# One core, attention into routed experts: a new table of priorities, group scores in one order of the array, value products by 64 columns, and small copies for two engines

## The chip, the core and the metric

One core of a Trainium2 chip runs the whole kernel. TensorE (PE in the rows, PEld for its loads of the stationary operand), VectorE (DVE), ScalarE (ACT) and GpSimd (POOL) each work through a list of instructions of their own, in a fixed order, and wait for each other by semaphores; SyncE (SP) issues most DMAs. The metric is the device time in microseconds from start to end of one execution.

## The reference, cut to what matters

The first half is attention over 8 batches of 8 heads, with 512 local and 32 global positions of 64 numbers each. Local rows see a band of 32 to either side and the global keys; global rows see all. The second half sends the result, as 544 rows of 512 numbers per batch, through four experts with causal attention, of which each row keeps two.

```python
s_g = scale * np.matmul(q_g, k_all.transpose(0, 1, 3, 2))
out_g = np.matmul(sm(s_g), v_all)
mask = np.abs(pos[:, None] - pos[None, :]) <= window          # window = 32
a_l = sm(np.concatenate([s_lg, np.where(mask, s_ll, -1e9)], axis=-1))
out_l = np.matmul(a_l, np.concatenate([v_g, v_l], axis=2))
...
for e in range(E):                                            # 4 experts, 2 of them kept per row
    q, k, v = x @ wq[e], x @ wk[e], x @ wv[e]
    ye = softmax(causal(scale * q @ k.transpose(0, 2, 1))) @ v @ wo[e]
    out += gate[e] * ye
```

All is float32. A float32 product stands in the rows of the trace as two instructions of TensorE, so a matmul of the program counts twice there; the projections split their operands into a high and a low part of a shorter type (`xh`, `xl`) and count once for each product of parts.

## The kernel before, in words

The 32 pairs of heads (8 batches of 4 pairs) go through the first half one after the other, in steps; the experts' work of a batch is laid between the pairs of later ones, and `step` writes down, for each step, what belongs to it. For pair k: `p1_load` and `p1_load_values` fetch it, `p1_trans` makes the transposed keys `kd` and queries `qp`, `p1_scores` (32 matmuls on tiles of 64 rows by 32 columns of the array) and `p1_softmax` make the banded weights, `p1_ptrans` turns them on TensorE, `p1_av` multiplies with the values `v` (tiles of 128 rows by 32 columns), `p1_turn` turns the result into `xh` and `xl`.

Around the values much is copied: `p1_load_values` builds overlapping windows of `v` from one loaded copy by six moves between partitions (`move`; one of them, of the last window alone, is small: 32x128) and three copies of the global values (`vg`). Before, all nine run on GpSimd, as do the copy of the global keys into `kd` in `p1_trans` and four copies `xt<-xh`, `xt<-xl` per batch in `m_v`. In a row of the trace they all bear the line of the helper `copy` (L417) or their own (L668, L1020).

Two pairs make a group, whose 128 global queries against 544 keys need a softmax of their own. In steps 1 and 3, and where the experts' tail rows of an older batch have scores in the same step, `long_scores` does it: 12 matmuls, four tiles of the array at a time. In the eight other groups `split_scores` (L838) cuts the keys into parts of 320 and 224 and lays them on all eight tiles at once; its softmax then has to swap minima and sums between the halves of the partitions (`swap`, L850) with small VectorE instructions, and has two exponentials on ScalarE (L860) for one (L934).

The experts of a batch: `m_v`, `m_qk` project (128x128 tiles), `m_gates` picks two of four, `m_scores`, `m_softmax`, `m_ptrans` as above, `m_av` (L1237) multiplies with the values in 32 columns of the array at a time, four tiles side by side, `m_out` and `m_out_tail` project and write 128x512 tiles; the last tile is written in two halves.

The order on each engine is no loop's: `Plan.op` writes down every operation with a duration that the author gives it and a priority (the step times 100, plus a shift from the table `SHIFT`), and `Plan.place` then plays the whole kernel through and fixes on every engine the order in which operations could start. An operation with two engines (`"ACT|DVE"`) gets the one that is free first. `SHIFT` is looked up by the function that an operation belongs to, its duration and its step.

Of the kernel before, what the change touches and what calls it, by code (L numbers as in the profile page):

```python
# [49 lines left out]
class Op:  # L50
    def __init__(self, k, engs, ns, fn, prio, packets, shape, slow, code, flow):
# [13 lines left out]
LAND = 650.0  # L65
# [10 lines left out]
SHARE = 800.0  # L76

SWITCH = {"scores": 198.0, "av": 114.0, "turn": 143.0}
# [10 lines left out]
    "clear_banks": {(3500, 100): -200},  # L89
    "evac": {(180, 100): -250, (180, 103): -50, (266, 110): 130, (266, 118): 120, (276, 116): 20,  # L90
        (316, 102): -110, (316, 108): 220, (369, 114): -120, (448, 103): 110, (475, 100): -240, (475, 102): -100,
        (475, 105): -90, (475, 106): -110, (475, 108): -140, (475, 112): -80, (475, 113): -70, (475, 135): 80},
    "high_low": {(264, 133): -100, (332, 104): -250, (332, 107): 140, (332, 111): 50, (332, 124): 160,
        (332, 130): -90, (332, 133): -70, (598, 113): 140, (598, 139): 250},
    "load": {(550, 100): -250, (550, 101): -250, (550, 102): -250, (550, 106): -220, (550, 108): -70,
        (550, 109): -70, (550, 123): -50, (550, 124): -140},
    "long_scores": {(60, 101): -240, (60, 103): -130, (60, 135): -200, (80, 111): -180, (80, 119): -50,
        (80, 127): -70, (80, 131): -90, (880, 101): -220, (880, 103): -170, (880, 111): -180, (880, 119): -50,
        (880, 123): -40, (880, 127): -20, (880, 131): -60, (880, 135): -250},
    "m_av": {(680, 141): -160, (1560, 141): -250, (2220, 113): -70, (2220, 115): -40, (2220, 117): -50,  # L100
        (2220, 121): -190, (2220, 123): -100, (2220, 125): -150, (2220, 127): 70, (2220, 129): -110,
        (2220, 133): -140, (2220, 135): -220},
    "m_gates": {(440, 115): -130, (440, 131): 180, (630, 115): 160, (1300, 111): 60},
    "m_qk": {(1504, 107): 80, (1504, 112): -60, (1504, 116): -10, (1504, 119): 10, (1504, 120): -70,
        (1504, 123): -50, (1504, 124): -30, (1504, 127): -120, (1504, 128): -20, (1504, 136): 250},
    "m_scores": {(431, 108): -100, (431, 110): 80, (431, 114): 30, (431, 116): 70, (431, 118): 50,
# [5 lines left out]
    "m_softmax": {(80, 120): -80, (80, 124): 80, (211, 111): -90, (211, 115): 140, (211, 133): -130,  # L112
# [4 lines left out]
    "m_tail_av": {(583, 113): 110, (583, 117): -50, (583, 121): 90, (583, 129): -10, (583, 133): -70,  # L117
        (583, 137): 190, (583, 141): -180},
    "m_tail_softmax": {(100, 131): 80, (110, 111): 150, (110, 119): 120, (610, 115): -90, (610, 119): -80,
        (610, 127): -30, (610, 139): -110, (745, 115): -110},  # L120
    "m_v": {(1440, 105): 50, (1440, 110): -150, (1440, 114): 60, (1440, 118): -50, (1440, 126): -90,
        (1440, 130): -40, (1440, 134): 250},
    "m_v_tails": {(330, 111): -60, (330, 119): 110, (1062, 111): -250},
    "out_tile": {(1400, 113): 60, (1400, 117): -80, (1400, 121): 150, (1400, 125): -110, (1400, 129): -100,
# [45 lines left out]
class Plan:  # L170
# [5 lines left out]
    def __init__(self):  # L176
        self.ops = []
        self.writers = {}
        self.prio = 0
# [183 lines left out]
def fused_kernel(ctx: ExitStack, tc: tile.TileContext, q_l, k_l, v_l, q_g, k_g, v_g,  # L363
# [1022 lines left out]
    def step(s):  # L1386
# [9 lines left out]
        def local():  # L1396
# [4 lines left out]
            elif group or tail is not None:  # L1401
                long_scores(group, tail)
# [120 lines left out]
```

## Time and profile before

| | |
|---|---|
| time, median of 3 runs | 463.72 us (463.31 to 464.33) |
| the profiled execution | 464.11 us, of which its span 462.3 us |
| busy: TensorE, VectorE, ScalarE, GpSimd | 443.6, 384.2, 329.4, 291.7 us |
| TensorE's granted clock | 1.0 of full speed throughout |

The profiled execution is 0.4 us above the median; 1.8 us of it lie around the span. TensorE is busy for 96% of the span, but "busy" holds pipelined instructions whose ends are modelled, so a stretch with full busy time can still hold gaps. How long a piece of TensorE's work takes is better read from the starts: from the first instruction of one piece to the first of the next.

### The profile page before, as it was taken

Reading aid. Unit: us, or ns where it says so; the run is one execution under the profiler, and the core shown is the slowest. Engines: PE = TensorE matmul, PEld = TensorE weight load, DVE = VectorE, ACT = ScalarE, POOL = GpSimd, SP = SyncE. Lnnn points to the kernel's source line nnn. Section 1 sums busy time; section 2 is a strip of 40 time slices with the busy share of each in tenths; the row PEclk is TensorE's granted clock in tenths of the full one; section 3 lists DMA queues with packets and bytes.
Section 4 is the critical chain, followed back from the end, with each engine's and each line's share of the span. In section 5 each row is a group of like instructions: output and inputs, shape, how many; then the busy total and the mean of one; then the engine's idle time right before and its main releaser. Section 6 shows DMA issues by size and latency. Waiting matters only on the chain.

```text
span 462.3 us, 25861 instructions
## 1 busy us (share of the span) xinstructions
PE 443.6 (96%) x10572; PEld 385.6 (83%) x10572; DVE 384.2 (83%) x1714; ACT 329.4 (71%) x1198; POOL 291.7 (63%) x563
## 2 busy tenths in 40 slices
PE   7877899999999999999999999999999999999996
PEld 5666789898879988789888898899978998798875
DVE  6997989999996997798988899598997986476681
ACT  4977759676886777786877688579678794563582
POOL 8899887998687559658409696744854931340420
PEclk9999999999999999999999999999999999999999
DMA  8786665865346345553135733653305000300023
GB/s 179 171 188 117 124 119 103 157 107 109 55 105 143 66 77 107 129 89 63 20 57 106 171 64 59 160 101 70 60 3 148 5 4 3 94 3 1 26 72 115
DMA packets 182535, 41.01 MB, mean 89 GB/s; under 512 B 177680, under 2 KB 177936, under 8 KB 182416
## 3 DMA queue, kind: packets, MB, share of 16 engines
q1 hardware_dynamic: 181840, 38.57, 40.6%
q8 instruction: 83, 1.36, 1.3%
q10 hardware_dynamic: 576, 0.79, 0.6%
q14 instruction: 36, 0.29, 0.2%
HBM read 30.42 MB, written 8.91 MB: 85 GB/s over the span
## 4 chain that ended last, share of the span: by engine, by line
PE 82%; DVE 6%; POOL 5%; issue 2%; SPq 2%; ACT 1%; DMA 1%; DVEq 0%; POOLq 0%; ACTq 0%
PE bank L998 20%; PE bank L739 11%; PE bank L1310 10%; PE bank L1029 9%; PE bank L1237 7%; PE bank L1151 6%; PE bank L769 6%; PE bank L706 5%; POOL v L417 5%; PE bank L968 2%; SPq L432 2%; PE bank L909 1%; PE bank L1291 1%; PE bank L838 1%; PE bank L800 1%
## 5 line engine op out<-in xcount | busy, mean ns | idle before, releaser
L417 POOL COPY v<-v 32x512 f32<-32x512 f32 (+3 forms) x192 | 114.3, 595 | 21.2 <-DMA v<-in_v_l_dram 11.7
L1186 POOL TENSOR_SCALAR pm<-pm,msm,gate 128x256 f32<-128x256 f32 (+3 forms) x124 | 74.7, 616 | 72.5 <-DVE msm L1175 24.9
L721 ACT ACTIVATE st<-st,sm 128x128 f32<-128x128 f32 x256 | 99.6, 392 | 16.4 <-DVE sm L718 16.3
L1170 ACT ACTIVATE pm<-pm,msm 128x128 f32<-128x128 f32 (+3 forms) x128 | 70.9, 557 | 26.0 <-DVE msm L1166 25.6
L417 POOL COPY v<-vg 32x640 f32<-32x640 f32 (+1 forms) x96 | 68.5, 714 | 11.7 <-issue 3.6
L718 DVE CUSTOM_DVE_ANT_0 st<-bank,band 128x128 f32<-128x128 f32 x256 | 58.0, 284 | 2.2 <-PE bank L706 1.8
L721 ACT ACTIVATION_READ_ACCUMULATOR st<-st,sm 128x1 f32 x256 | 48.6, 190 | 0.0
L706 PE MATMUL bank<-kd,qp 64*32 64x128 f32 x2048 | 39.4, 272 | 2.5 <-issue 1.4
L1166 DVE CUSTOM_DVE_ANT_0 pm<-bank,cmask 128x512 f32<-128x512 f32 (+1 forms) x64 | 38.0, 612 | 3.1 <-PE bank L1151 2.9
L1151 PE MATMUL bank<-kt,qt 64*32 64x480 f32 (+15 forms) x1024 | 38.7, 394 | 0.5 <-issue 0.5
L998 PE MATMUL bank<-xh,wk_hi 128*128 128x272 f32 x128 | 38.6, 302 | 0.0
L769 PE MATMUL bank<-v,ptw 128*32 128x64 f32 x2048 | 35.6, 220 | 3.0 <-POOL v L417 2.0
L706 PEld LDWEIGHTS bank<-kd,qp 64*32 64x32 f32 x2048 | 33.0, 105 | 6.3 <-issue 3.6
L1029 PE MATMUL bank<-wv_hi,xh 128*128 128x260 f32 x128 | 37.2, 291 | 0.0
L998 PE MATMUL bank<-xl,wk_hi 128*128 128x272 f32 x128 | 37.0, 289 | 0.0
L998 PE MATMUL bank<-xh,wq_hi 128*128 128x272 f32 x128 | 37.0, 289 | 0.0
L998 PE MATMUL bank<-xh,wq_lo 128*128 128x272 f32 x128 | 36.9, 289 | 0.0
L998 PE MATMUL bank<-xh,wk_lo 128*128 128x272 f32 x128 | 36.8, 288 | 0.0
L998 PE MATMUL bank<-xl,wq_hi 128*128 128x272 f32 x128 | 36.8, 287 | 0.0
L769 PEld LDWEIGHTS bank<-v,ptw 128*32 128x32 f32 x2048 | 31.4, 110 | 6.2 <-POOL v L417 2.6
L1029 PE MATMUL bank<-wv_lo,xh 128*128 128x260 f32 x128 | 36.3, 283 | 0.0
L1029 PE MATMUL bank<-wv_hi,xl 128*128 128x260 f32 x128 | 36.1, 282 | 0.1
(194 smaller groups left out, 1300.5 us busy)
## 6 DMA issues: line engine op xcount, KB each, us to landing
v<-in_v_l_dram SPq DMA_DIRECT2D x64, 120.0 KB, 3.0
kn<-in_k_l_dram SPq DMA_DIRECT2D x104, 64.0 KB, 2.5
qn<-in_q_l_dram SPq DMA_DIRECT2D x104, 64.0 KB, 2.5
out_dram<-ot SPq DMA_DIRECT2D x66, 64.0 KB, 1.7
out_dram<-ot SPq DMA_DIRECT2D x14, 256.0 KB, 2.4
v<-in_v_l_dram SPq DMA_DIRECT2D x32, 64.0 KB, 2.7
kn<-in_k_l_dram SPq DMA_DIRECT2D x12, 128.0 KB, 3.2
qn<-in_q_l_dram SPq DMA_DIRECT2D x12, 128.0 KB, 3.3
```

What stands on the lines that cost most here:

```text
L417: ENG[e].tensor_copy(out, in_)
L706: nc.tensor.matmul(sp[h].t[32 * g:32 * g + 32, 128 * t:128 * t + 128], qp.t[rows, 32 * u:32 * u + 32], kd.t[rows, c:c + 128], start=True, ...
L718: op("DVE", 211, lambda e, h=h, t=t, i=i: nc.vector.tensor_tensor_reduce(out=st.t[:, h, t], in0=sp[h].t[:, 128 * t:128 * t + 128], in1=ban ...
L721: op("ACT", 385, lambda e, h=h, t=t, i=i: nc.scalar.activation(st.t[:, h, t], st.t[:, h, t], AF.Exp, bias=sm.t[:, 0, i:i + 1], scale=-1.0, ...
L739: nc.tensor.transpose(two[y].t[:, k, :], block()[rows], ident[rows, rows])
L769: nc.tensor.matmul(xq.t[32 * g:32 * g + 32, t, h, :], pt.t[:, h, 32 * u:32 * u + 32], v.t[:, h, window(u), :], start=True, stop=True)
L998: nc.tensor.matmul(pp.t, w[:, ch, cols], x(part, ch)[:, n], start=(ch == 0 and w is hi and part == 0), stop=(ch == NCH - 1 and part == 1))
L1029: nc.tensor.matmul(pv.t, x(part, ch)[:, 128 * i:128 * i + 128], w[:, ch, :], start=(ch == 0 and part == 0 and w is hi), stop=(ch == NCH - ...
L1151: nc.tensor.matmul(sp[x].t[32 * g:32 * g + 32, at:at + n], qt.t[rows, q0:q0 + 32], kt.t[rows, :n], start=True, stop=True)
L1170: op("ACT", 280 + 0.83 * n, lambda e, x=x, at=at, n=n, s=s: nc.scalar.activation(pm.t[:, x, at:at + n], pm.t[:, x, at:at + n], AF.Exp, bia ...
L1186: lambda e, x=x, at=at, n=n, row=row, s=s: ENG[e].tensor_scalar(pm.t[:, x, at:at + n], pm.t[:, x, at:at + n], sm.t[:, 3, s:s + 1], gate.t[ ...
L1310: nc.tensor.matmul(po.t, lhs(part, c), w[:, c, :], start=(c == 0 and part == 0 and w is hi), stop=(c == 1 and part == 1))
```

## The change

It has five parts.

1. `SHIFT` is a new table. Its keys name an operation more closely: helpers (`evac`, `load`, `turn_halves`, ...) by the function that they serve (`owner`), and on TensorE and SyncE also by how many of the same kind came before in the step (`#0`, `#1`). The table's numbers are new, and so are many of the durations and constants by which `Plan.place` plays the kernel through.
2. `split_scores` is gone; all groups go through `long_scores` and `p1_global_softmax`.
3. `m_av` takes 64 columns of the array at a time: half as many matmuls, two tiles side by side.
4. The small window move, the copy into `kd` and the four `xt` copies may go to GpSimd or VectorE.
5. The multiply of the experts' weights keeps its engines, but has other durations in the plan.

```diff
 SHIFT = {
-    "clear_banks": {(3500, 100): -200},
+    "clear_banks#0": {(3500, 100): -160},
+    "evac into long_turn": {(316, 120): -70, (316, 126): -110},
...
-        kind = fn.__code__.co_qualname.split(".<locals>.")[1]
+        kind = owner(fn)
         step = int(self.prio // 100)
+        key = kind, round(ns[0]), step
+        if engs[0] in ("PE", "SP"):
+            self.seen[key] = self.seen.get(key, -1) + 1
+            kind += f"#{self.seen[key]}"
...
-            op(*spread(252 + 0.79 * 128 * cols, 2 * D * cols), f, r=[(v, key)], w=[(v, ("m", to, slots.start, frm))], late=120)
+            engs, ns = spread(252 + 0.79 * 128 * cols, 2 * D * cols) if cols > 1 else ("POOL|DVE", (655, 200))
+            op(engs, ns, f, r=[(v, key)], w=[(v, ("m", to, slots.start, frm))], late=120)
...
-        op("POOL", 380, lambda e: nc.gpsimd.tensor_copy(
-            groups(kd.t)[:, :, 96:], kq.t[:, p:p + 1, :SG].to_broadcast([128, n3, SG])), r=[kq], w=[(kd, "g")])
+        op("POOL|DVE", (640, 240), lambda e: copy(
+            e, groups(kd.t)[:, :, 96:], kq.t[:, p:p + 1, :SG].to_broadcast([128, n3, SG])), r=[kq], w=[(kd, "g")])
...
-    def split_scores(b, g):
...
-        op("PE", 580, f, r=[kq, *kdl], w=sps, shape="scores", code=64, flow=0.8)
...
-                    op("POOL", 300, lambda e, g=g, k=k, part=part: nc.gpsimd.tensor_copy(
-                        xt.t[:, 2 * g:2 * g + 2, b % 2, k, :], X[b, g, part].t[:, :, SL:]), r=[X[b, g, part]],
+                    op("POOL|DVE", (540, 150), lambda e, g=g, k=k, part=part: copy(
+                        e, xt.t[:, 2 * g:2 * g + 2, b % 2, k, :], X[b, g, part].t[:, :, SL:]), r=[X[b, g, part]],
...
-                            for d in range(0, D, 32):
-                                nc.tensor.matmul(yp.t[64 * x + d:64 * x + d + 32, at:at + width],
-                                                 vt.t[:, j, 64 * (2 * c + x) + d:64 * (2 * c + x) + d + 32],
-                                                 pt.t[:, x, 2 * j:2 * j + width // 128, :].rearrange("p s q -> p (s q)"),
-                                                 start=(j == 0), stop=(j == big))
+                            nc.tensor.matmul(yp.t[64 * x:64 * x + 64, at:at + width],
+                                             vt.t[:, j, 64 * (2 * c + x):64 * (2 * c + x) + 64],
+                                             pt.t[:, x, 2 * j:2 * j + width // 128, :].rearrange("p s q -> p (s q)"),
+                                             start=(j == 0), stop=(j == big))
...
-            if group and tail is None and s >= 5:
-                split_scores(*group)
-            elif group or tail is not None:
+            if group or tail is not None:
                 long_scores(group, tail)
```

Over the whole program VectorE gets 21 of the 32 small moves, 12 of the 32 copies into `kd` and 15 of the 32 `xt` copies; with `split_scores` 40 small VectorE instructions go (64 of its own against 24 of the one softmax, the two evacuations left out on both sides). TensorE's tile shape changes 173 times instead of 166; away from the 64x32 shape of the scores it changes 36 times instead of 39.

Here is GpSimd, early in the program, at the values of the fourth pair, the last of the first batch; `kd_77` is the key tile of a later pair, `cmask` a mask of the experts, `xt` a copy that waits for the first group's result. Before:

```order
L417 COPY v<-vg 32x10x64 x2
L417 COPY v<-vg 32x2x4x64
L417 COPY v<-v 32x10x64 x2
L417 COPY v<-v 32x2x4x64
L417 COPY v<-v 32x2x64
L417 COPY v<-v 32x2x4x64
L417 COPY v<-v 64x2x4x64
L668 COPY kd_77<-kq 128x5x32
```

And after, up to the same last move of that pair:

```order
L478 COPY v<-vg 32x10x64 x2
L478 COPY kd_77<-kq 128x5x32
L567 MEMSET cmask 128x512
L568 AFFINE_SELECT cmask<-cmask 128x128
L478 COPY xt<-xh 128x2x32
L478 COPY xt<-xl 128x2x32
L478 COPY v<-v 32x10x64 x2
L478 COPY v<-v 32x2x4x64 x2
L478 COPY v<-v 64x2x4x64
```

The small move (32x2x64) has left the row, as in the three pairs ahead; the mask, which before stood in front of all values, and two `xt` copies have come in front of the last moves.

TensorE at the third group, before (`kd_78` and `kd_79` are its two pairs' keys; the rows go on in this manner to 16):

```order
L838 MATMUL bank_68<-kd_78,kq 32x192
L838 MATMUL bank_70<-kd_78,kq 32x32
L838 MATMUL bank_68<-kd_79,kq 32x192
L838 MATMUL bank_70<-kd_79,kq 32x32
L838 MATMUL bank_68<-kd_78,kq 32x192
L838 MATMUL bank_70<-kd_78,kq 32x32
```

After, where the same group's keys are `kd_78` and `kd_77`, and the score tile of a pair follows at once:

```order
L903 MATMUL bank_66<-kd_78,kq 32x128 x2
L903 MATMUL bank_66<-kd_77,kq 32x128 x2
L903 MATMUL bank_66<-kd_78,kq 32x384 x2
L903 MATMUL bank_66<-kd_77,kq 32x384 x2
L768 MATMUL bank_68<-kd_77,qp 32x128
```

The wide half of the group stands alone in four matmuls of 128 and four of 384 columns; its last four, of 32 columns, stand elsewhere in the row.

ScalarE at the very end, before:

```order
L415 COPY ot<-bank_69 128x512
L1324 DMA out_dram<-ot 128x512
L1324 DMA out_dram<-ot 32x512 x2
L415 COPY ot<-bank_64 128x256
L1319 DMA out_dram<-ot 128x256
```

After:

```order
L476 COPY ot<-bank_71 128x512
L1324 DMA out_dram<-ot 32x512 x4
L476 COPY ot<-bank_70 128x256
L1319 DMA out_dram<-ot 128x256
L1324 DMA out_dram<-ot 128x512
```

The tile that is written in halves is no longer the last: a whole tile, evacuated by VectorE in one piece, is issued behind it.

## Rows read from the trace of the kernel before

**Rows 1.** Busy time by stretch: us, PE, PEld, DVE, ACT, POOL, clock, DMA.

```profile
0.00:42.00 42.00, 32.84 (x983) 24.90 (x983) 34.66 (x158) 30.48 (x115) 37.50 (x82) 1.00 0.78 169
42.00:140.00 98.00, 94.41 (x2352) 84.03 (x2356) 92.62 (x423) 73.21 (x281) 82.69 (x152) 1.00 0.59 110
140.00:380.00 240.00, 238.51 (x5940) 211.86 (x5939) 208.10 (x950) 182.97 (x677) 152.19 (x293) 1.00 0.40 81
```

**Rows 2.** TensorE in order of time: start, us, what, [idle before <- releaser]; early.

```profile
9.96 1.13 PE L901 MATMUL bank<-kd,kq 64*32 64x32 f32 x24
11.02 0.66 PE L676 MATMUL bank<-ident,kn 128*128 128x128 f32 x4
12.05 1.16 PE L706 MATMUL bank<-kd,qp 64*32 64x128 f32 x64
13.13 0.71 PE L739 MATMUL bank<-ident,st 64*128 64x64 f32 x16
...
37.25 1.03 PE L769 MATMUL bank<-v,ptw 128*32 128x64 f32 x57 [1.38 <-POOL v L417]
...
41.60 0.38 PE L706 MATMUL bank<-kd,qp 64*32 64x128 f32 x2 [0.38 <-issue]
```

**Rows 3.** GpSimd in order of time, the first 40 us.

```profile
6.26 0.52 POOL L506 MEMSET cmask<- 128x512 f32 x1
...
9.20 1.91 POOL L417 COPY v<-vg 32x512 f32<-32x512 f32 x3 [0.17 <-DMA vg<-in_v_g_dram]
11.17 0.32 POOL L668 COPY kd<-kq 128x160 f32<-128x160 f32 x1
...
12.96 7.63 POOL L417 COPY v<-v 32x640 f32<-32x640 f32 x12 [0.70 <-DMA v<-in_v_l_dram]
...
29.14 4.21 POOL L417 COPY v<-vg 32x640 f32<-32x640 f32 x3
...
37.52 0.23 POOL L1020 CAST xt<-xh 128x64 fp32r<-128x64 f32 x1
```

**Rows 4.** TensorE in order of time, from 60 us.

```profile
62.52 1.16 PE L706 MATMUL bank<-kd,qp 64*32 64x128 f32 x64
63.42 0.83 PE L838 MATMUL bank<-kd,kq 64*32 64x192 f32 x32
63.96 1.42 PE L1151 MATMUL bank<-kt,qt 64*32 64x416 f32 x32
...
78.97 0.66 PE L739 MATMUL bank<-ident,st 64*128 64x64 f32 x16
79.46 0.88 PE L739 MATMUL bank<-ident,pm 64*128 64x64 f32 x16
...
84.12 0.40 PE L706 MATMUL bank<-kd,qp 64*32 64x128 f32 x2 [1.05 <-issue]
```

**Rows 5.** Waits of TensorE: who for whom, us in total, times, longest.

```profile
PEld bank L1237 <- issue: 1.8, 5, 0.8
...
PE bank L739 <- ACT long L860: 1.2, 1, 1.2
```

**Rows 6.** The chain that ended last: start, us, what.

```profile
105.20 2.16 PE bank L1237 x48
```

**Rows 7.** VectorE and GpSimd at 67.4 us, in order of time.

```profile
67.39 0.72 POOL L417 COPY v<-vg 32x640 f32<-32x640 f32 x1
...
67.41 0.73 DVE L724 TENSOR_SCALAR sm<-sm 128x8 f32<-128x8 f32 x1
```

**Rows 8.** Groups by shape: count, busy us, mean ns of one, idle before.

```profile
L724 DVE TENSOR_SCALAR sm<-sm 128x8 f32<-128x8 f32 x32 | 9.7, 302 | 3.3 <-ACT st L721 3.3
...
L417 POOL COPY v<-v 32x128 f32<-32x128 f32 x32 | 9.3, 292 | 1.8
```

**Rows 9.** DMA issues: count, KB each, us from issue to landing.

```profile
out_dram<-ot ACTq DMA_DIRECT2D x1, 256.0 KB, 2.1
...
out_dram<-ot ACTq DMA_DIRECT2D x1, 128.0 KB, 1.8
```

More of the change, by code (lines that the diff above doesn't have):

```diff
@@ L64 @@
 START = 500.0
-LAND = 650.0
+LAND = 700.0
 AGAIN = 700.0
@@ L75 @@
 HELD = 150.0, 400.0
-SHARE = 800.0
-SWITCH = {"scores": 198.0, "av": 114.0, "turn": 143.0}
+SHARE = 500.0
+SWITCH = {"scores": 225.0, "av": 114.0, "turn": 143.0}
 ENTER = 105.0
@@ L95 @@
[L95 to L102, printed above, removed]
@@ new lines @@
+    "evac into long_turn": {(316, 120): -70, (316, 126): -110},
+    "evac into p1_ptrans": {(475, 102): -210},
+    "evac m_ptrans": {(369, 112): -150, (369, 140): -250},
+    "evac out_tile": {(475, 129): 80},
+    "evac p1_batch_turn": {(262, 110): -40, (262, 126): -90},
+    "evac p1_trans": {(180, 101): -140, (448, 100): 60, (448, 101): -190, (448, 102): -160, (448, 103): 30,
+        (475, 102): -250, (475, 103): -190},
+    "high_low m_av": {(477, 137): -30, (598, 133): -250},
[24 rows of a table added]
+    "m_gates": {(450, 119): 250, (630, 131): 250, (700, 119): 110},
[13 rows of a table added]
@@ new lines, with owner @@
+    "m_softmax": {(211, 111): 40, (211, 123): 70, (211, 139): 30, (344, 128): 140, (386, 125): 140,
[4 rows of a table added]
+    "m_tail_softmax": {(100, 123): 140, (110, 119): -30, (610, 127): 20},
[4 rows of a table added]
+    "m_v_tails": {(444, 119): -60},
[34 rows of a table added]
+    "setup": {(1165, 102): 250},
+    "setup_masks": {(900, 105): 20},
[23 rows of a table added]
+}
+HELPERS = "load", "evac", "high_low", "turn_halves", "into", "turned"
+def owner(fn):
+    name = fn.__code__.co_qualname.split(".<locals>.")[1]
+    if name in HELPERS:
+        for cell in fn.__closure__ or ():
+            inner = cell.cell_contents
+            inner = inner[0] if isinstance(inner, list) and inner else inner
+            if hasattr(inner, "__code__"):
+                inner = owner(inner)
+                if inner not in (*HELPERS, "copy"):
+                    return f"{name} {inner}"
+    return name
@@ L527, in order @@
                 nc.gpsimd.memset(before[:, x, :x], 1.0)
-        for name, ns, f in (("before", 700, order), ("rmask", 1550, reversed_blocks), ("cmask", 900, upper),
-                            ("tmask", 1150, last)):
+        for name, ns, f in (("before", 700, order), ("rmask", 2000, reversed_blocks), ("cmask", 900, upper),
+                            ("tmask", 1700, last)):
             op("POOL", ns, f, w=[name], late=50)
@@ L650, in p1_load_values @@
             rows = slice(96 - 32 * first, 128 - 32 * first)
-            op(*spread(218 + 0.845 * 128 * nw, 2 * D * nw), lambda e, first=first, nw=nw, rows=rows: copy(
+            op(*spread(185 + 0.845 * 128 * nw, 2 * D * nw), lambda e, first=first, nw=nw, rows=rows: copy(
                 e, v.t[rows, :, first:NW:3, :], vg.t[:, 2 * p:2 * p + 2, :].unsqueeze(2).to_broadcast([32, 2, nw, D])),
@@ L804, in unit @@
                 rows = slice(64 * h, 64 * h + 64)
[L805 removed]
+                op("ACT", 220, lambda e, rows=rows, h=h: nc.scalar.copy(hi()[rows], tt.t[rows, :, h ^ flip, :]), r=[tt],
                    w=[(hk[0], (hk[1], h))])
                 op("DVE", 222, lambda e, rows=rows, h=h: nc.vector.tensor_sub(
[L808 removed]
+                    lo()[rows], tt.t[rows, :, h ^ flip, :], hi()[rows].bitcast(F32)), r=[tt, (hk[0], (hk[1], h))],
@@ L956, in p1_global_av @@
     def p1_global_av(b, g):
-        pt, sm, col, at, view = (G[b, g][x] for x in ("pt", "sm", "factor", "at", "view"))
+        pt, sm = G[b, g]["pt"], G[b, g]["sm"]
         vs = [PR[b * NP + 2 * g + j]["v"] for j in range(2)]
@@ L971, in p1_global_av @@
         x = [X[b, g, name] for name in ("xh", "xl")]
-        G[b, g]["turn"] = turned(xg, lambda: sm.t[:, col:col + 1],
+        G[b, g]["turn"] = turned(xg, lambda: sm.t[:, 5:6],
                                  ((lambda: x[0].t[:, :, :SG], (x[0], "g")), (lambda: x[1].t[:, :, :SG], (x[1], "g"))),
-                                 [(sm, col)], view)
+                                 [(sm, 5)], flip=g)
     M = {}
@@ L1118, in tail @@
                 nc.vector.tensor_copy(gt.t[32 * x:32 * x + 32], gx[:32, 4:, x])
-        op("DVE", 580 if odd else 350, first, r=some, w=[(tmp, "x0")], late=10)
+        op("DVE", 700 if odd else 330, first, r=some, w=[(tmp, "x0")], late=10)
         op("ACT", 130, lambda e: nc.scalar.activation(parts()[4], parts()[4], AF.Exp), r=[(tmp, "x0")],
@@ L1235, in f @@
                         for x in range(2):
-                            for d in range(0, D, 32):
-                                nc.tensor.matmul(yp.t[64 * x + d:64 * x + d + 32, at:at + width],
-                                                 vt.t[:, j, 64 * (2 * c + x) + d:64 * (2 * c + x) + d + 32],
-                                                 pt.t[:, x, 2 * j:2 * j + width // 128, :].rearrange("p s q -> p (s q)"),
-                                                 start=(j == 0), stop=(j == big))
-            op("PE", 20 + 220 * sum(2 * big + 1 for big in some), f, r=[vt, *pts], w=[yp], shape="av", code=16 * sum(big + 1 for big in some))
+                            nc.tensor.matmul(yp.t[64 * x:64 * x + 64, at:at + width],
+                                             vt.t[:, j, 64 * (2 * c + x):64 * (2 * c + x) + 64],
+                                             pt.t[:, x, 2 * j:2 * j + width // 128, :].rearrange("p s q -> p (s q)"),
+                                             start=(j == 0), stop=(j == big))
+            op("PE", 20 + 220 * sum(2 * big + 1 for big in some), f, r=[vt, *pts], w=[yp], shape="half", code=8 * sum(big + 1 for big in some))
             high_low(lambda part, n0=n0, n=n: y[part].t[:, c, n0:n0 + n], lambda yp=yp: yp.t, n, [yp],
```

107 lines of the change are left out of this document (14 added, 93 removed), and 145 rows, old and new, of the table SHIFT.

## The prediction

> **What bounds the kernel now.** I read first the table of busy time by stretch [rows 1]. TensorE bounds: it runs at the full granted clock throughout, and its idle time is small wherever the two halves of the program overlap. Up to 42 us it is idle for 42.0 − 32.8 = 9.2 us; from 42 to 140 us for 3.6; from 140 to 380 us for 1.5. VectorE is nearly as full in the middle stretch (92.6 of 98, so 5.4 us of slack) and has room later (208 of 240). GpSimd is fullest in the first stretch (37.5 of 42). So a change pays in three ways only: less work on TensorE's own line, an earlier start of the experts' work, or fewer of the waits left.
>
> Next TensorE in order of time, since a busy share does not tell how long a piece takes; I take each piece from its own first start to the start of the next [rows 2, 4]. Then GpSimd for the first 40 us [rows 3]: from 12.96 us it copies values one behind the other, and at 37.25 us TensorE had waited 1.38 us for the last of them before it could multiply the fourth pair [rows 2], behind which, after the scores at 41.60, the first projection of the experts stands. The list of waits shows what belongs to `split_scores` [rows 5]: one wait of 1.2 us of the turns for its exponentials (L860). Two further idle pieces with nobody named stand where its matmuls had just met a score tile, 0.38 us at 41.60 and 1.05 us at 84.12 [rows 2, 4].
>
> **The change part by part.** The sum is made against the profiled run, 464.1 us; it is 0.4 us above the median, and the difference is applied to the median, 463.7.
>
> *Group scores.* A group in one order took from 9.96 to 11.02, 1.06 us [rows 2]. That holds a change of tile shape: a score tile that is followed by its own shape took 62.52 to 63.42 = 0.90 us [rows 4], and one that is followed by another shape 12.05 to 13.13 = 1.08 [rows 2], so 0.18 is the change. The group alone is then 1.06 − 0.18 = 0.88. The split took 63.42 to 63.96 = 0.54 [rows 4]. Eight groups at 0.88 − 0.54 = 0.34 are **+2.7 us**; if the split's 0.54 held a change of shape too, more, up to +3.3, which I take as the upper end. All of this lies on the bound engine.
>
> *Tile shapes.* By the order there are three changes fewer away from the scores (0.18 each, −0.5) and ten more of other kinds, which I price between nothing and the same 0.18 (up to +1.8). I take +0.1 each, so **+0.5 us**, between −0.5 and +1.3.
>
> *Value products of the experts.* 48 instructions of 32 columns, four tiles side by side, took 2.16 us [rows 6]; there are 16 such pieces. Now 24 instructions of 64 columns, two side by side: the same columns in the same number of rounds. The nearest row for two halves of the array at once is a turn: 16 instructions from 78.97 to 79.46 = 0.49 us [rows 4], though it halves the rows, not the columns. Scaled by the length of the operands that would make up to 2.45 us a piece, 16 × 0.29 = +4.6 at worst. On the other side, the loads of this line waited 1.8 us in five places with no releaser named [rows 5], and the number of loads is halved, so up to −1.8. I take **−0.5**, near the row of the piece itself, as the work per column is the same.
>
> *Start of the experts' work.* On GpSimd before the fourth pair's last move, four small moves (0.29 each [rows 8]) and one copy into `kd` (0.32 [rows 3]) go, −1.5. In front come the mask (0.52 [rows 3], and the selection, which I price like the 128x160 copy, 0.32) and two `xt` copies (0.23 each [rows 3]), +1.3. The 0.70 us that it waited at 12.96 for the first values [rows 3] can be filled with copies of the global values, −0.7. That is **−0.9 us** on the chain that ends in the fourth pair's product. Three copies of `vg` at 29.14 took 4.21 us [rows 3] where three others took 1.91 at 9.20, so some 2.2 us of it are no work of theirs. If the new place avoids half of that it is −2.0. If the `xt` copies make GpSimd wait for the first group's result, which it may, the gain goes and some time is lost: +0.5.
>
> *The waits of the split.* 1.2 + 0.38 + 1.05 = **−2.6 us** if all go [rows 2, 4, 5]. What is late next is the chain of the one softmax: its exponential (L934) covers 544 keys, where the first of the two covered 320. Its matmuls stand earlier in front of its turns than before by the order, which is the cover; if the cover is not there, the term is nothing. Ends −2.6 and 0.
>
> *Copies on VectorE.* It gets 48 copies over the program, against 40 small instructions that go. At the mean of a small one, 0.30 us [rows 8], that is 14.4 against at most 12. By the order some 19 of the copies fall between 42 and 140 us: 5.7 us, in a stretch with 5.4 of slack, where the split's own go as well. GpSimd is off the path there, so what it gains is worth nothing by itself. I take **+0.5**, between 0 and +2.9 (half of the 19 stand in front of a result that TensorE waits for). The cover is VectorE's idle time, and it is thin before 140 us.
>
> [...] At 67.41 us an instruction of VectorE on 128x8 numbers took 0.73 us: a copy of GpSimd had begun 0.02 us ahead and ran 0.72 [rows 7]; the mean of that form is 0.30 [rows 8]. [...]
>
> *Looser order.* Apart from the waits of the split, TensorE's idle time from 42 to 380 us is 3.6 + 1.5 − 1.2 − 1.05 = 2.8 us [rows 1, 4, 5]. By the pieces' durations laid along the new order, there is more of TensorE's own work between a producer and its consumer: turned weights and their product have under 2.5 us between them in 7 pairs of 32, before in 12; the product and its turn in 10, before in 14. I take 0.4 of the 2.8: **−1.2**, between −2.8 and 0.
>
> *End.* The last tile issued is now a whole one: 256 KB landed in 2.1 us, the half of 128 KB in 1.8 [rows 9]: **+0.3**. The loads' own priorities move DMAs on SyncE's queue, which I cost at nothing: the DMA engines are 0.40 busy after 140 us [rows 1], and a pair's tensors are asked for a step ahead; if that cover went, a load would show as a wait of TensorE for `kn`.
>
> **Sum:** +2.7 + 0.5 − 0.5 − 0.9 − 2.6 + 0.5 − 1.2 + 0.3 = −1.2, so **462.5 us**. Its terms are small, and of both signs; none is known to better than a microsecond.
>
> **The rivals.** *Most of it works out.* The start gains its 2.0, all of the 2.8 goes, and the loads of the experts' products no longer wait: −1.1 − 1.6 − 1.3 beyond the forecast, 458.5 us. For it: the order is looser at each place that I compared. Against it: it needs three ends at once.
>
> *Half given back: the same.* Half of the split's waits come back behind the one softmax, +1.3: 463.8. For it: five waits of one kind seldom vanish without one of another.
>
> *Slower: a new wait takes the place of the split's.* The scores cost their 2.7 for certain, since they lie on the bound engine; the 2.6 comes back as waits of the turns for L934, the 2.8 stay as they are, and the ten changes of shape cost their full price: −1.2 + 2.6 + 1.2 + 0.8 = +3.4, 467.1 us. It decides once TensorE waits for the one softmax, all groups together, for more than 1.5 us. For it: one long exponential on one engine instead of two on shorter parts, a fuller VectorE in front of it.
>
> *Slower: the shared port.* If each of the 19 copies between 42 and 140 us takes the 0.73 of [rows 7], they make 13.9 us on an engine with 5.4 of slack: +8.5 in place of my +0.5, 470.5 us. Against it: VectorE's stall of this kind is the rare case, since its mean for that small form is 0.30, and GpSimd has fewer copies to run beside it.
>
> *Not side by side.* If two tiles of 64 columns ran one behind the other, the 2.16 would double 16 times: +34.6, 497 us. No row shows this form; nothing speaks for it but that.
>
> *It does not do what it says.* Small copies could all have stayed with GpSimd; the order shows 48 that moved, so this has no chance.
>
> **How the numbers follow.** The forecast with its neighbourhood (460.5 to 462.8) gets 0.31, most of it works out 0.16, the same 0.23, the new wait 0.22, the shared port 0.06, not side by side 0.02. A measurement of this kernel can tell 0.2%, 0.9 us, from no change. So faster by over that is 0.31 + 0.16 = 0.47, within it 0.23, slower by over it 0.22 + 0.06 + 0.02 = 0.30. The range leaves out the last two, 0.08, and the outer parts of the best and the slower case, some 0.05 each: 457.3 to 467.6. Alone, the forecast's own range is 460.5 to 464.5.
>
> **What the profile after would show.** TensorE's starts: a group alone 0.85 to 1.0 us, the experts' products near 2.1 a piece. Waits: L860's gone, those for L934 under 1.5 us in total. GpSimd: the fourth pair's last move ends by about 36.4 us in place of 37.25, and the first projection starts about 0.9 us earlier than now. By stretch: TensorE's idle from 42 to 140 us near 2, VectorE's busy time there under 95. The prediction is wrong if the time of a group is not 0.34 more than the split's, if `xt` copies hold up GpSimd in the first 40 us, or if VectorE's small copies take 0.5 us and more on average. The chain of waits should still be TensorE's for over 80%; if it runs through VectorE between 42 and 140 us, the port rival is the one.

## The result and the profile after

| | before | after |
|---|---|---|
| median | 463.7 us (463.3 to 464.3) | 469.9 us (469.1 to 470.4) |
| profiled execution, its span | 464.1, 462.3 us | 469.8, 468.1 us |
| ratio to before, 95% interval | | 1.0131 (1.0112 to 1.0149) |

The change makes the kernel 6.2 us slower. The forecast was 462.5, its upper end 467.6.

First the busy time by stretch, the answer to [rows 1]: us, PE, PEld, DVE, ACT, POOL, clock, DMA.

```profile
0.00:42.00 42.00, 34.04 (x893) 27.10 (x898) 35.68 (x159) 30.87 (x118) 34.74 (x73) 0.92 0.79 169
42.00:140.00 98.00, 95.23 (x2258) 82.13 (x2242) 91.80 (x407) 71.25 (x266) 74.52 (x128) 0.98 0.56 105
140.00:380.00 240.00, 236.90 (x5627) 211.13 (x5626) 210.46 (x947) 173.73 (x638) 146.88 (x272) 1.00 0.40 83
```

TensorE's idle time is 8.0, 2.8 and 3.1 us where it was 9.2, 3.6 and 1.5, so over the whole span it is even a little shorter (468.1 − 450.0 = 18.1 against 18.7). The loss stands under "busy", 450.0 for 443.6. That is a column to be read with care. The granted clock of this execution is not 1.0 throughout, as it was in the profiled one of before; that is not the change's doing alone, since other executions of before show means of 0.99 to 1.00 too. And one reads more from starts than from busy time. From the first start of each piece to the first start of the next, without the idle time between, TensorE's work has grown by 7.0 us: the scores of groups and tail rows take 19.3 us in all for 15.4 (18.7 to 19.7 in four other traces of after's order), the experts' value products 37.0 for 35.9. The projections of queries and keys take 101.2 for 99.6 and the first turns of keys and queries 7.9 for 6.7, but these two move from one execution to the next (99.6 to 100.3 and 7.1 to 8.4 in the same four traces). The rest is small and of both signs.

Here is TensorE from 63 us on (start, us, what, [idle before <- releaser]):

```profile
63.12 1.13 PE L903 MATMUL bank<-kd,kq 64*32 64x32 f32 x24 [0.30 <-DVE xn L835]
64.18 0.46 PE L801 MATMUL bank<-ident,xn 64*128 64x64 f32 x8
65.83 0.82 PE L801 MATMUL bank<-ident,st 64*128 64x64 f32 x16 [1.19 <-DVE sm L780]
66.78 0.77 PE L969 MATMUL bank<-v,longt 128*32 128x64 f32 x40
67.48 0.50 PE L999 MATMUL bank<-xh,wq_hi 128*128 128x272 f32 x1
67.78 0.43 PE L999 MATMUL bank<-xh,wq_lo 128*128 128x272 f32 x1
68.00 0.43 PE L999 MATMUL bank<-xl,wq_hi 128*128 128x272 f32 x1
```

A group alone takes 63.12 to 64.18 = 1.06 us, as [rows 2] had it. Then TensorE waits 1.19 us for a mask of scores on VectorE, and the projections behind that start 0.22 to 0.30 us apart. What GpSimd and VectorE did just before, from the order of time of all engines:

```profile
62.73 3.42 POOL L478 COPY v<-v 32x640 f32<-32x640 f32 x5
...
63.49 0.78 DVE L478 COPY v<-v 32x128 f32<-32x128 f32 x1
64.30 0.64 DVE L478 COPY kd<-kq 128x160 f32<-128x160 f32 x1
64.86 0.27 DVE L780 CUSTOM_DVE_ANT_0 st<-bank,band 128x128 f32<-128x128 f32 x1
```

Two of the moved copies stand in front of the mask and take 0.78 and 0.64 us while GpSimd copies without a break; the mask that TensorE needs comes up to 0.78 + 0.64 = 1.4 us later than without them. And behind the gap the clock falls, by the busy time of two microseconds each (columns as above):

```profile
64.00:66.00 2.00, 0.81 (x15) 0.50 (x12) 1.97 (x13) 0.77 (x4) 1.84 (x4) 1.00 0.65 124
66.00:68.00 2.00, 1.86 (x58) 1.63 (x58) 2.00 (x13) 2.00 (x11) 1.86 (x4) 0.90 0.66 109
68.00:70.00 2.00, 2.00 (x10) 2.00 (x10) 2.00 (x8) 2.00 (x7) 1.82 (x4) 0.50 0.61 102
70.00:72.00 2.00, 2.00 (x15) 2.00 (x14) 1.92 (x8) 1.72 (x8) 1.88 (x4) 0.74 0.53 88
```

TensorE, busy for 0.81 of the 2.00 us from 64 on, is granted 0.50 of its clock from 67.6 to 71.0 us, and twelve matmuls of a projection, which last 1.71 us elsewhere in the chain that ended last, take 2.92 (start, us, what):

```profile
67.55 2.92 PE bank L999 x12
...
116.80 1.71 PE bank L999 x12
```

Another run of after, at a granted clock of 1.00, took 470.4 us, so the clock does not decide the whole.

The waits of TensorE that are new (who for whom, us in total, times, longest):

```profile
PE bank L801 <- DVE xn L835: 2.3, 3, 1.4
PE bank L738 <- DMA qn<-in_q_l_dram: 1.9, 1, 1.9
PE bank L831 <- POOL v L478: 1.6, 1, 1.6
...
PE bank L801 <- DVE sm L780: 1.2, 1, 1.2
PE bank L831 <- DVE msm L1167: 1.1, 2, 0.9
PE bank L768 <- DVE ptu L478: 0.9, 1, 0.9
```

None is for the exponential of the one softmax, which the forecast's rival named. They are mostly VectorE's: TensorE's waits for it come to 8.5 us, in before to 4.7. Waits of its matmuls with no releaser named, 3.0 us in five places in before, are gone from this list.

### The profile page after: what moved, and what is told of

Read it like the earlier page. It is cut to its first block, busy times and chain, and to the rows that moved or that the text cites. A ratio compares the mean times of both kernels' runs of the same rounds, so it can differ in the third digit from the quotient of the medians.

```text
span 468.1 us, 24844 instructions
## 1 busy us (share of the span) xinstructions
PE 450.0 (96%) x10124; PEld 391.6 (84%) x10124; DVE 394.6 (84%) x1732; ACT 324.4 (69%) x1172; POOL 278.5 (60%) x515
## 4 chain that ended last, share of the span: by engine, by line
PE 77%; DVE 8%; DMA 6%; ACT 2%; POOL 2%; SPq 2%; issue 2%; DVEq 0%; POOLq 0%; ACTq 0%
PE bank L999 19%; PE bank L801 10%; PE bank L1310 10%; PE bank L1030 8%; PE bank L1237 6%; PE bank L1152 6%; PE bank L831 5%; PE bank L768 5%; DMA v<-in_v_l_dram 4%; SPq L493 2%; PE bank L969 2%; POOL v L478 2%; PE bank L903 2%; ACT st L783 1%; DVE st L780 1%
## 5 line engine op out<-in xcount | busy, mean ns | idle before, releaser
L478 POOL COPY v<-v 32x640 f32<-32x640 f32 (+3 forms) x171 | 109.1, 638 | 19.8 <-DMA v<-in_v_l_dram 11.3
L783 ACT ACTIVATE st<-st,sm 128x128 f32<-128x128 f32 x256 | 99.6, 393 | 15.4 <-DVE sm L780 15.2
L1171 ACT ACTIVATE pm<-pm,msm 128x512 f32<-128x512 f32 (+3 forms) x128 | 70.8, 555 | 26.7 <-DVE msm L1167 26.4
L478 POOL COPY v<-vg 32x640 f32<-32x640 f32 (+1 forms) x96 | 67.2, 700 | 21.4 <-issue 10.6
L1152 PE MATMUL bank<-kt,qt 64*32 64x128 f32 (+15 forms) x1024 | 40.0, 394 | 0.0
L768 PEld LDWEIGHTS bank<-kd,qp 64*32 64x32 f32 x2048 | 34.0, 108 | 4.8 <-issue 1.3
L831 PEld LDWEIGHTS bank<-v,ptw 128*32 128x32 f32 x2048 | 30.4, 110 | 6.6 <-DVE msm L1167 2.1
```

What stands on the lines that cost most here:

```text
L478: ENG[e].tensor_copy(out, in_)
L768: nc.tensor.matmul(sp[h].t[32 * g:32 * g + 32, 128 * t:128 * t + 128], qp.t[rows, 32 * u:32 * u + 32], kd.t[rows, c:c + 128], start=True, ...
L783: op("ACT", 385, lambda e, h=h, t=t, i=i: nc.scalar.activation(st.t[:, h, t], st.t[:, h, t], AF.Exp, bias=sm.t[:, 0, i:i + 1], scale=-1.0, ...
L831: nc.tensor.matmul(xq.t[32 * g:32 * g + 32, t, h, :], pt.t[:, h, 32 * u:32 * u + 32], v.t[:, h, window(u), :], start=True, stop=True)
L1152: nc.tensor.matmul(sp[x].t[32 * g:32 * g + 32, at:at + n], qt.t[rows, q0:q0 + 32], kt.t[rows, :n], start=True, stop=True)
L1171: op("ACT", 280 + 0.83 * n, lambda e, x=x, at=at, n=n, s=s: nc.scalar.activation(pm.t[:, x, at:at + n], pm.t[:, x, at:at + n], AF.Exp, bia ...
```

## The experiments

A planner that lays a new order for each edit can't tell what one part costs. So in all kernels below the order is written out: the list of all 3323 operations with their engines, as the planner of before (or of after) laid it, stands in the kernel and is followed. Then one thing is changed. In the kernel where that is only the cut of TensorE's first matmuls in two, the rows of VectorE, ScalarE and GpSimd are those of before, one for one. Each result is a ratio to before on the same chip; before's own median there was 463.3 to 464.4 us.

| order of | edit | ratio (95%) |
|---|---|---|
| before | groups in one order, 12 matmuls | 1.0226 (1.0201 to 1.0252) |
| before | value products by 64 columns | 1.0207 (1.0179 to 1.0234) |
| before | 48 copies on VectorE | 1.0131 (1.0095 to 1.0167) |
| before | all three | 1.0236 (1.0209 to 1.0263) |
| before | first matmuls cut in eight | 1.0636 (1.0604 to 1.0669) |
| before | 64 columns, as many instructions as before | 1.0043 (1.0024 to 1.0062) |
| before | one order, as many instructions as before | 0.9996 (0.9969 to 1.0023) |
| before | the last two and the copies on VectorE | 1.0092 (1.0057 to 1.0127) |
| before | 48 copies on ScalarE | 1.0028 (1.0007 to 1.0049) |
| before | first matmuls cut in two | 1.0037 (1.0017 to 1.0057) |
| after | 48 copies back on GpSimd | 1.0103 (1.0085 to 1.0121) |
| after | 48 copies on ScalarE | 1.0096 (1.0062 to 1.0130) |
| after | two `xt` copies later | 1.0137 (1.0116 to 1.0158) |
| after | first matmuls cut in two | 1.0126 (1.0084 to 1.0167) |
| before | early small copies on ScalarE | 0.9979 (0.9956 to 1.0002) |
| before | that, and one order with 16 matmuls | 0.9971 (0.9951 to 0.9992) |

### One form at a time, and a surprise

Theory: the forms cost what the trace of after shows (2 us for the products, the copies' waits). Rival: the forms are cheap and the new order is the bad one.

```diff
-            if group and tail is None and s >= 5:
-                split_scores(*group)
-            elif group or tail is not None:
+            if group or tail is not None:
```

> The kernel before with its own order written out, in which only the form of the eight split groups is changed: the twelve matmuls of the one order stand where the split's stood, and the one softmax's instructions where the split's stood. If the score form costs what the rows of before gave (0.34 a group) and the split's waits come back behind the one softmax: +2.7, 466.4 us. If the waits of the split (2.6 us) go with it, as the prediction had it: 463.8 us.

Measured 474.3 us.

```diff
-                            for d in range(0, D, 32):
-                                nc.tensor.matmul(yp.t[64 * x + d:64 * x + d + 32, at:at + width],
+                            nc.tensor.matmul(yp.t[64 * x:64 * x + 64, at:at + width],
```

> The kernel before in its own order, with only the experts' value products in 64 columns. The prediction had -0.5: 463.2 us. The trace of after shows 2.31 us a piece where before had 2.16 to 2.19; if that is the form itself, 16 x 0.12 to 0.15 = +2: 465.7 us.

Measured 473.2 us.

```diff
 ORDER = """
-... 31g ... 15g ...
+... 31d ... 15d ...
```

(A number is an operation, the letter its engine; so for all 48.)

> The kernel before in its own order, with only the 48 small copies moved to VectorE, each at the place where it stood among all engines' operations. The prediction had +0.5: 464.2 us. If they wait for GpSimd's running copies (0.6 to 0.8 us in place of 0.2, as at 63.49 and 64.30 us of after) in front of what TensorE needs: 466 us and more, and TensorE's granted clock falls after the gaps. If GpSimd's relief at the start is worth something: under 463.2.

Measured 470.0 us.

> All three forms of after (one order of group scores, 64 columns, 48 copies on VectorE) in the order of before. If the forms make the loss, 469 to 470 us, as after. If the new order makes it, this lies at 465 to 467 us, at the sum of the three kernels beside it.

Measured 474.5 us. Each form alone loses 6.7 to 11 us, all three together hardly more than the dearest one. Neither theory had that. TensorE in the kernel with only the 64 columns shows what happens, at 302 us (start, us, what):

```profile
302.55 0.77 PE L1422 MATMUL bank<-vt,longt 128*32 128x64 f32 x40
303.13 0.73 PE L901 MATMUL bank<-v,ptw 128*32 128x64 f32 x37
305.93 0.64 PE L901 MATMUL bank<-v,ptw 128*32 128x64 f32 x27 [2.07 <-issue]
```

After 37 of 64 matmuls of one operation, which wait for nothing that the others don't, TensorE stands still for 2.07 us. In the trace of the same kernel, DMA traffic from 303.2 to 305.9 us holds one packet of `q8`, a queue that the profile lists under the kind `instruction`. It lasts from 303.4 to 304.5 us, and TensorE goes on 1.4 us behind its end:

```profile
q8 instruction: 1, 0.02, 2.7%
```

The page of before shows the whole queue (packets, MB, share), and above it busy time and instructions of each engine:

```profile
PE 443.6 (96%) x10572; PEld 385.6 (83%) x10572; DVE 384.2 (83%) x1714; ACT 329.4 (71%) x1198; POOL 291.7 (63%) x563
...
q8 instruction: 83, 1.36, 1.3%
```

(10572 + 10572) / 83 = 255 instructions a packet; after has 79 packets for 20248, 256; the kernel with the groups in one order has 82 for 21016, 256, and the one with 64 columns 80 for 20376, 255. By size a packet of before is 1.36 MB / 83 = 16.4 KB. I read this as TensorE's program coming in packets of 256 instructions, of which short matmuls use one up faster than the next is there; that is an inference, and what the kept traces of all 18 kernels show for it is this: of 71 idle pieces of TensorE over 0.3 us with no releaser named, 67 end 1.2 to 1.7 us behind the end of a packet of this queue; of 188 with one named, 22 do. By that reading an edit that changes the number of instructions moves every later place where a packet ends.

The planner has this in its model, which the prediction overlooked: `Plan.stream`, the same in both kernels, plays TensorE's program as coming in blocks of `CODE = 256` instructions, and the order is laid around their arrival. An order that is written out and then edited is no longer laid around it; the order of after, laid anew, is.

### Is it the place of the packets?

```diff
-                nc.tensor.matmul(bank.t, zero.t[:, :128], zero.t, start=True, stop=True)
+                for x in range(0, 512, 64):
+                    nc.tensor.matmul(bank.t[:, x:x + 64], zero.t[:, :128], zero.t[:, x:x + 64], start=True, stop=True)
```

> The kernel before, same order, same work: only the eight matmuls of 512 columns that clear the banks at the start, before any data are there, are cut into 64 of 64 columns. That puts some 112 instructions more in front of everything TensorE does, and so moves every place at which its next packet of 256 instructions (16 KB each, 83 of them) is used up. If the losses of the three kernels of one form come from the supply of TensorE's instructions, which its order was laid around, this loses 3 to 10 us too, with idle time of no releaser in the middle of short matmuls. If they come from the forms and their waits, it stays within 1 us of before.

Measured 493.2 us, 29.8 more. Of these, 10 are direct: the 64 matmuls last 13.9 us, where the eight took some 3.7. The other 20 are not; TensorE's waits with no releaser are 15.3 us in 22 places, the largest (us in total, times, longest):

```profile
PE bank L901 <- issue: 6.0, 7, 2.0
PE bank L1423 <- issue: 3.0, 2, 1.6
PE bank L871 <- issue: 3.0, 5, 1.1
```

Since the direct part blurs it, the same cut with 256 columns, 16 instructions more in the same time:

> The kernel before, same order and work; only the eight matmuls that clear the banks are cut in two (256 columns each), 16 instructions more at the very start, in the same time there. If a small change of the place of TensorE's instruction packets costs, it is 1 to 4 us slower, with waits of no releaser among short matmuls; if only large moves cost, 463.6 us.

> The same cut of the first eight matmuls in the kernel after, in its own order. If its order is laid around the packets like the one of before, 1 to 4 us slower than after: 471 to 474 us. If packets already hit it where they lie now, no change or faster: 468 to 470 us.

Measured +0.37% in the order of before, and in the order of after no difference from after itself (1.0126, after 1.0131), though its interval, 1.0084 to 1.0167, is too wide to exclude one of the same 0.4%. Sixteen instructions that do nothing new cost before 1.7 us; its waits with no releaser rise from 3.0 us to 4.8. The cleanest answer comes from the forms with as many instructions as before:

```diff
+                    parts = [(j, 0, 128) for j in range(big)] + [(big, 0, 64), (big, 64, 128)]
+                    parts += [(j, 128, 256) for j in range(big)]
+                    for j, lo, hi in parts:
...
+                            nc.tensor.matmul(yp.t[64 * x:64 * x + 64, at + lo:at + hi],
```

> The kernel before, same order, value products in 64 columns, but with the moving columns in halves, so that each piece has as many instructions as before. If the 9.9 us of the kernel with 64 columns came from the place of the instruction packets, that goes: 463 to 466 us, and what is left is the form itself (16 pieces). If the form or its waits cost that much, 470 us and more.

```diff
+                    elif part and cut:
+                        for c in (0, 2):
+                            nc.tensor.matmul(
+                                o_[:, 128 + 96 * c:320 + 96 * c].rearrange("p (c s) -> p c s", s=96), kq.t[rows, 2 * g + j, SG:],
```

> The kernel before in its own order, the eight split groups in the one order, but with the wide part cut so that a group has 16 matmuls as the split has: TensorE's instruction packets stay where they were. If the form costs 0.34 a group and the softmax's waits come back: +2.7, 466.3 us. If the split's waits of 2.6 go with it: 463.7 us. If the 11 us of the kernel with 12 matmuls were no matter of packets: 470 us and more.

Measured 465.1 us (+1.6) and 463.6 us (none). With the count of instructions kept, 8.3 of the 9.9 us of the products and all 11 of the scores are gone. TensorE's waits with no releaser go the same way: 10.0 us (groups) and 9.8 (products) with fewer instructions, 2.4 and 2.1 with as many as before. That a loss comes with the count and goes with it is shown, and 67 of the 71 idle pieces end 1.2 to 1.7 us behind a packet; no run changes the supply alone.

The 1.6 us are not all the 64 columns' own. A piece takes 2.31 us with them, and 2.36 in this kernel, where its moving columns are cut as well:

```profile
142.82 2.36 PE bank L1369 x48
```

> All three forms of after in the order of before, with both score groups and value products cut so that TensorE has as many instructions as before; the 48 copies stand on VectorE. If the forms add up without packets: 466.3 for the scores, 1.6 for the products, and the copies' 6.5: about 474 us at most; if the copies' loss was partly a shifted place of the packets in time, 469 to 471 us. At 466 us the order of after would be the worse one.

Measured 468.2 us, +0.92% or some 4.3 us: less than the parts added up (0 + 1.6 + 6.7 = 8.3 us), and less than the 6.2 of after, though the two intervals overlap.

### The copies

If it is GpSimd that makes VectorE's copies long, ScalarE may do better from the same place in the row:

```diff
 ORDER = """
-... 31g ... 15g ...
+... 31a ... 15a ...
```

> The kernel before in its own order, with the same 48 copies on ScalarE in place of VectorE, each at the same place. If the 6.7 us of the kernel with them on VectorE come from copies that wait for GpSimd's running copy, this loses clearly less (464 to 466 us), and the copies take their 0.2 to 0.3 us. If any engine beside GpSimd is too full to take them in its row, this loses as much: 469 us and more.

Measured 464.7 us, +0.28%, against +1.31% for the same copies on VectorE; TensorE does the same work in the same order in both, and in before. In the kernel with the copies on VectorE one of them reads:

```profile
67.62 0.72 POOL L549 COPY v<-vg 32x640 f32<-32x640 f32 x1
...
67.64 0.81 DVE L549 COPY kd<-kq 128x160 f32<-128x160 f32 x1
```

It began 0.02 us behind GpSimd's copy and ended 0.11 behind it, the picture of [rows 7]. By shape, the twelve copies into `kd` took in that kernel (x count | busy us, mean ns | idle before):

```profile
L549 DVE COPY kd<-kq 128x160 f32<-128x160 f32 x12 | 5.0, 431 | 0.4 <-ACT kq L547 0.4
```

And in the kernel with them on ScalarE:

```profile
L547 ACT COPY kd<-kq 128x160 f32<-128x160 f32 x12 | 3.7, 317 | 0.0
```

The mean differs by a tenth of a microsecond only; the price is in a few. On ScalarE none of the 48 took over 0.33 us. On VectorE 15 took 0.45 to 0.82 us, and each of these began while an instruction of GpSimd ran and ended 0.05 to 0.11 us behind its end. So these copies end with GpSimd's instruction; why they do, no run shows. Between the two kernels lie 1.0%, some 5 us. How much of the 5 us comes from VectorE being the fuller engine (384 us busy in before, ScalarE 329), these runs do not part.

In the order of after, the copies back to GpSimd and on to ScalarE:

> The kernel after in its own order written out, with the 48 copies put back on GpSimd, each at its place; TensorE's stream is unchanged. If VectorE's copies that wait for GpSimd's make the loss: 465 to 467 us, without the gap at 64 us and the low clock behind it. If the loss is the order and the forms: 469 to 471 us, or more since GpSimd's own work comes later.

> The kernel after in its own order, with its 48 copies on ScalarE in place of VectorE. If in this order too the copies cost by waiting for GpSimd's running copy, this gains what the ones on GpSimd gained or more: 466 to 468.5 us, and the gap of TensorE at 64 us is gone. If the order has been laid around copies on VectorE, no gain: 469.9 us or more.

Both 1.0% over before, some 0.3% under after (468.5 and 468.6 us). The gap at 64 us is gone in both, as the busy time of that stretch shows for ScalarE's:

```profile
64.00:66.00 2.00, 2.00 (x53) 1.91 (x51) 1.51 (x6) 2.00 (x9) 1.30 (x3) 1.00 0.79 143
```

So in after's own order the copies cost some 1.5 us, not 5 to 7; that order was laid with them on VectorE. Both intervals, 1.0085 to 1.0121 and 1.0062 to 1.0130, overlap after's, so even the 1.5 is not clear of noise.

### The start of the experts' work

In after, GpSimd, in order of time, waits for both `xt` copies' data before the fourth pair's last moves:

```profile
30.95 0.24 POOL L478 CAST xt<-xh 128x64 fp32r<-128x64 f32 x1 [1.32 <-ACT xh L487]
31.96 0.24 POOL L478 CAST xt<-xl 128x64 fp32r<-128x64 f32 x1 [0.77 <-DVE xl L488]
32.26 4.34 POOL L478 COPY v<-v 32x640 f32<-32x640 f32 x5
```

```diff
 ORDER = """
-... 396g ... 397g ... 139g ... 144g ...
+... 139g ... 144g 396g 397g ...
```

> The kernel after in its own order, but the first two xt copies, for whose data GpSimd waited 2.1 us at 30 us, stand behind the fourth pair's moves. If that wait sets the start of the experts' work, it comes 1.5 to 2 us earlier: 468 us. If VectorE and ScalarE are as late by themselves, no change: 469.9 us.

Measured 470.3 us, no gain. Its trace shows why, on GpSimd at the same place:

```profile
30.38 4.32 POOL L610 COPY v<-v 32x640 f32<-32x640 f32 x5 [1.04 <-DMA v<-in_v_l_dram]
```

GpSimd now waits for the load of `v` instead, and starts its moves 1.9 us earlier; the first projection starts at 42.4 us for 42.9 in after (before: 42.0). Loads, ScalarE and VectorE are all late there. The rival held. Nor does that start decide the whole: with the copies back on GpSimd it comes at 43.7 us, in a kernel that is no slower than after.

In the order of before GpSimd's row was late for the fourth pair by 1.38 us [rows 2]. Eleven of its copies there, four moves and seven into `kd`, go to ScalarE:

```diff
 ORDER = """
-... 15g ... 53g ... 31g ...
+... 15a ... 53a ... 31a ...
```

> The kernel before in its own order, with only the small copies (four moves, six copies into kd) of the first 37 us on ScalarE. If GpSimd's row of values sets the start of the experts' work, that comes up to 1.2 us earlier: 462.3 us. If other waits take its place, or TensorE's packets are hit, 463.5 us or more.

> The kernel before in its own order with two of the parts that cost nothing: the small copies of the first 37 us on ScalarE, and the groups in the one order with 16 matmuls each. If the gains of the two (some 1.2 us, and the split's waits) stand beside each other: 461 to 462.5 us, under both kernels. If not: 463.6 us.

Measured 462.4 us (its interval just touches 1) and, with the groups in one order at 16 matmuls, 463.3 us beside 464.4 for before on that chip: 0.3% faster, the only kernel here whose interval lies wholly under 1, though not by more than the first alone. In the first one's profiled execution the experts' first projection starts 0.8 us earlier than in before:

```profile
41.20 0.36 PE L1161 MATMUL bank<-wv_hi,xh 128*128 128x260 f32 x1
```

In before the same row starts at 41.99 us.

## Why the prediction was wrong, step by step

The sum let TensorE's idle time shrink by 4.7 us (the split's waits 2.6, the looser order 1.2, the start 0.9) and its work grow by some 2.7 (scores 2.7, shapes 0.5, products −0.5). In the two profiled executions idle time shrank by 0.6 us and busy time grew by 6.4. So the step that failed most is that the waits would go: 4.1 of the 7.4 us between forecast and result. New ones took their place, above all for VectorE (8.5 us for 4.7) and for `qn` (1.9). The next is the work on TensorE, mis-sized in the scores and in the products.

*Group scores, +2.7, and the split's waits, −2.6.* Together +0.1, and that is what the two gave in the order of before at an equal count of instructions (463.6 us for 463.6); there all scores together take 18.4 us for 15.4, +3.0. In after, a group of 1.06 us, with the change of shape behind it, is as priced and no wait for L934 came, but all scores take 19.3, +3.9, over the upper end of 3.3 (which by its own figures, 8 × (0.88 − 0.36), should have been 4.2). And 1.43 of the 2.6 us was read wrongly: the idle pieces at 41.60 and 84.12 end 1.3 to 1.6 us behind a packet of `q8`, and in the order of before with the split gone an idle piece of 0.87 us still ends at 42.41 us. Right as a pair in before's order, in part by luck; in after not.

*Value products, −0.5.* Wrong: +1.1 us by the starts, up to 1.6 by the run. I took the one piece at 2.16 us; the chain of before holds as many at 2.30. After's take 2.31 each, as in its chain of work (start, us, what; before's, then after's):

```profile
284.16 2.30 PE bank L1237 x48
...
129.91 2.31 PE bank L1237 x24
```

I also read the 1.8 us of waits without a releaser as this line's own and let the halved loads remove them. With 64 columns in before's order 1.2 us of them are still there, in three places, so the number of loads is not what makes them.

*Tile shapes, +0.5; end, +0.3.* Not tested one by one.

*Start, −0.9.* Wrong: 0.9 later. The bound of +0.5, that the `xt` copies make GpSimd wait, came true with 2.1 us; and what I costed at nothing, the loads' new priorities, shows as the 1.9 us that TensorE waits for `qn` before 12.97 us. Since moving the `xt` copies back gave nothing, that term was no single cause.

*Copies on VectorE, +0.5, and the rival at 0.06, in which each copy takes 0.73 us.* Wrong, and most so in the order of before: there they alone cost 6.7 us, of which ScalarE's run leaves 1.1 to 1.3. I priced them at VectorE's idle time and let the mean of 0.30 us speak against the long case, though [rows 7] showed it in the trace. No run shows the port that the rival is named for; the kernel with the copies on VectorE showed 15 of 48 at 0.45 to 0.82 us. The mean, 0.35 us in after, says little: what counts is what stands behind the one copy that is long, as behind those of 0.78 and 0.64 us at 63.49 and 64.30 us. In after itself they cost some 1.5 us, 1.0 over the term; VectorE's busy time from 42 to 140 us is 91.8, and TensorE holds 77% of the chain of waits. So the rival's time, 470.5, came out by luck, not by its sum.

*Looser order, −1.2.* Wrong. TensorE's idle time from 42 to 380 us rose from 5.1 to 5.9 us, where the forecast left 1.6. Distances in TensorE's own work don't tell whether VectorE is in time.

What is left: after without copies on VectorE is still 1.0% over before, of which the products hold 0.2 to 0.4%. The other 0.6% or more, some 3 us, comes with its order. The place of the packets is not what costs there, as far as idle time shows it: TensorE's list of waits in after has none without a releaser. That the scores' 3.9 us come without the waits going is the nearest that the traces say; no run parts it further. The forms in before's order (1.0057 to 1.0127) and after (1.0112 to 1.0149) even overlap a little, so how much worse the new order itself is stays open.

## What to carry to other kernels

Before a form is compared with another in an order that stays as it is, keep the number of instructions on the engine that bounds: in the order of before, which its planner laid around the blocks of its model, 16 more at the start cost 0.37%, and an edit cost nearly five times what its form did (2.07% and 0.43% for the products). In after, whose order was laid anew, that price did not show: none of the waits of TensorE's matmuls there is without a releaser, where before had 3.0 us of them. Such a wait belonged here to a place in the program and not to the line it is booked under: 67 of 71 ended 1.2 to 1.7 us behind a packet of `q8`. And a small copy for VectorE beside a GpSimd that copies all the time is priced by what stands behind it: the 48 cost 1.31% there, and 0.28% on ScalarE, a fifth of that.

## What was not expected of the hardware

The packets of the queue `q8` keep step with TensorE's instructions, 83 for 21144 in before and 79 for 20248 in after, 255 and 256 a packet, and with 64 columns in the order of before TensorE stood still for 2.07 us in the middle of one operation and went on 1.4 us behind the end of a packet. In after, from 64 to 66 us, TensorE was busy for 0.81 of 2.00 us, and from 67.6 to 71.0 us the granted clock was 0.50.
